# Transposing ten of sixteen token tiles with block-moving DMAs and VectorE instead of TensorE

## The chip, the cores and the metric

The kernel runs on one core of a Trainium2 chip, as one launch. The metric is the device time in microseconds (us) of one execution. Times within the kernel are counted from the start of the profiled span.

## The reference

```python
def _A_ref(x, wqkv, wo):                      # H = 32 heads of Dh = 16, W = 8, dil = 2
    q, k, v = split(x @ wqkv)
    idx = pos[:, None] - arange(W) * dil      # each token looks at itself and 7 tokens before, every second one
    logits = einsum("bhsd,bhswd->bhsw", q, k[idx]) * Dh ** -0.5
    logits = where(idx >= 0, logits, -1e9)
    o = einsum("bhsw,bhswd->bhsd", softmax(logits), v[idx])
    return o @ wo

def _B_ref(x, w1, b1, w2, b2):
    return relu(x @ w1 + b1) ** 2 @ w2 + b2

xn = _layernorm(A_x)                          # S = 2048 tokens, D = 512, F = 1792, all float32
out = A_x + _A_ref(xn, A_wqkv, A_wo) * _silu(_B_ref(xn, B_w1, B_b1, B_w2, B_b2))
```

## The kernel before

The 2048 tokens are 16 tiles of 128. Every product is made of three passes over high and low parts (`PASSES`), each operand split into a rounded high part (ScalarE, `AF.Copy`) and the remainder (a subtraction on VectorE or GpSimd). A product of one tile with one third of wqkv is 12 matmuls of 128x512.

**Stage 1** walks the tiles in pairs (a, b), a = 2, 4, ... 14; this text calls one turn of that loop a step, and (t, s) the product of tile t with third s (0 = q, 1 = k, 2 = v). A step has six products, in the order (a,0) (b,0) (a,1) (b,1) (a,2) (b,2). While it runs, the tiles of the next step are transposed, and x of the step after that is normalised:

- `mean`, `spread` and `norm` (L345, L350, L357) are the layernorm of a tile from tile 2 on: two passes of ScalarE with an accumulated sum, small operations on GpSimd, and a third pass that writes `xn`. `norm(t)` also issues the load of x of tile t + 4.
- `trans` (L376) transposes `xn` on TensorE in four blocks of 128x128 into the PSUM tile `pxT`, and ScalarE copies it to the high part of `xt`; `lowx` (L384) makes the low part on VectorE.
- `qkv` (L390) makes the product in one of four PSUM accumulators (`psA`, 4 buffers); ScalarE evacuates it to `stg`, and per pair one DMA stores it to DRAM (`sq`, `sk`, `sv`). With b stored, the pair's `xt` goes to `sx` in DRAM, for stage 2.
- `weights` loads w1 and w2 by slices f (`load_w`) through four buffers in turn (`piece`), and splits them later (`split_w`: two copies on ScalarE, two subtractions on GpSimd).

The windowed attention is a stream for VectorE (`attention`, L205), by units of 256 tokens: q, k and v of a unit are loaded back from DRAM (`load_u`), four pairs of a 128x2048 product and a reduction make the logits, softmax follows, and four more pairs make the output, stored to `so`. `pump` (L300) decides how much of this stream is put between the products: it keeps a clock for TensorE and one for VectorE, with a price for each instruction (227 ns a matmul, 150 a transpose, VectorE by elements), and issues attention until VectorE's clock is `LATE` = 3 us ahead of TensorE's. The engines' instructions then stand in the order in which they were written (`Ordered`); DMAs are placed on SP's queue by the scheduler of the language, and SP issues them strictly one after another.

**Stage 2** runs over four chunks of 512 tokens and 14 slices f: `up` (x by w1, relu, square; TensorE and ScalarE), `lowh` (the low part of h, on VectorE), `down` (h by w2), beside the rest of the attention; then the output of the attention is transposed on VectorE in 32x32 blocks (`trans_o`, L589), multiplied by wo, gated with silu and added to x. up(0,0) and up(0,1) stand already in the last step of stage 1.

Two things lie in memory where the change touches them: `zero` (L168), 14 rows that are stored ahead of k's and v's first tokens, has its own place, and so has `b2t` (L182), which is loaded in stage 1.

Of the kernel before, what the change touches and what calls it, by code (L numbers as in the profile page):

```python
# [8 lines left out]
F32 = mybir.dt.float32  # L9
FR = mybir.dt.float32r  # L10
AF = mybir.ActivationFunctionType
# [3 lines left out]
P = 128  # L15
S = 2048
D = 512
F = 1792
KT = D // P
# [4 lines left out]
HALO = (W - 1) * DIL  # L24
# [5 lines left out]
BI = 8  # L30
# [6 lines left out]

WARM = 18
WARM2 = 3

MATMUL, TRANSPOSE, DVE_FIXED, SLACK, LATE, ROOM = 227, 150, 170, 500, 3000, 1000

# [2 lines left out]
def body(ctx: ExitStack, tc: tile.TileContext, x, wqkv, wo, w1, b1, w2, b2, out):  # L45
# [3 lines left out]
    clock = {"PE": 0.0, "V": 0.0}  # L49
# [28 lines left out]
    PE, V, A, G = Ordered(nc.tensor, "PE"), Ordered(nc.vector, "V"), Ordered(nc.scalar), Ordered(nc.gpsimd)  # L78

    def not_before(t):  # L80
        clock["V"] = max(clock["V"], t)

    dma = nc.sync.dma_start

    const = ctx.enter_context(tc.tile_pool(name="const", bufs=1))
    dram = ctx.enter_context(tc.tile_pool(name="dram", bufs=1, space=bass.MemoryType.DRAM))
    att = ctx.enter_context(tc.tile_pool(name="att", bufs=1))
# [5 lines left out]
    def psA(name):  # L93
        return psum.tile([P, 512], F32, name=name, tag="acc", bufs=4)
# [4 lines left out]
    def psT(name):  # L99
        return psum.tile([P, 512], F32, name=name, tag="tp", bufs=2)  # L100
# [14 lines left out]
    ident = const.tile([P, P], F32, name="ident")  # L115
# [6 lines left out]
    px, pstg, pwq, pxT = (p1ctx.enter_context(tc.tile_pool(name=n, bufs=1)) for n in ("px", "pstg", "pwq", "pxT"))  # L122
    xins = {}
# [6 lines left out]
    def load_x(t):  # L130
        xins[t] = px.tile([P, D], F32, name=f"x{t}", tag="x", bufs=4)
        dma(xins[t], tile_rows(x, t))
# [32 lines left out]
    mhalf = const.tile([P, 1], F32, name="mhalf")  # L165
    G.memset(mhalf, -0.5)
    mask = const.tile([P, BI, W], F32, name="mask")
    zero = px.tile([HALO, 4, P], F32, name="zero")  # L168

    def constants():  # L170
        G.memset(zero, 0.0)
        for t in (sk, sv):
            dma(t[:, :HALO, :].rearrange("g h c -> h g c"), zero)
        G.memset(mask, 0.0)
        for blk in (1, 0):
            for w in range(W):
                n = max(0, min(BI, (W - 1 - w) * DIL - blk * BI))
                if n:
                    G.memset(mask[:4 * blk + 4, :n, w], -1e9)

    b1t = const.tile([P, NF], F32, name="b1t")
    b2t = const.tile([P, D], F32, name="b2t")  # L182

    sq = dram.tile([4, S, P], F32, name="sq")
    sk = dram.tile([4, HALO + S, P], F32, name="sk")
# [114 lines left out]
    def pump(margin=-SLACK):  # L300

        limit = clock["PE"] + margin
        while True:
            if coming[0] is None:
                coming[0] = next(stream, None)
            if coming[0] is None or clock["V"] + coming[0] > limit:
                break
            coming[0] = next(stream, None)
        if coming[0] is None:
            not_before(limit)  # L310
# [13 lines left out]
    def split_w(f):  # L324
        for i, r in enumerate(raws.pop(f)):
            split(w12[f][:, 0, i], w12[f][:, 1, i], r, G)


    NT = S // P
    mv, means, rs, shifts, xn, pTs, xt, xT, seen = {}, {}, {}, {}, {}, {}, {}, {}, {}  # L330

    def moments(t, st):
        mv[t] = px.tile([P, 2], F32, name=f"mv{t}", tag="mv", bufs=2)
# [5 lines left out]
    def small(name, t):  # L339
        return px.tile([P, 1], F32, name=f"{name}{t}", tag=name, bufs=3)  # L340

    def scratch(t):
        return px.tile([P, D], F32, name=f"scratch{t}", tag="scratch")

    def mean(t):  # L345
        means[t] = small("mean", t)
        A.activation(scratch(t), xins[t], AF.Copy, accum_out=means[t])
        G.tensor_scalar(means[t], means[t], -1.0 / D, None, op0=OP.mult)

    def spread(t):  # L350
        rs[t], shifts[t] = small("rs", t), small("shift", t)
        A.activation(scratch(t), xins[t], AF.Square, bias=means[t], accum_out=rs[t])
        G.tensor_scalar(rs[t], rs[t], 1.0 / D, 1e-5, op0=OP.mult, op1=OP.add)
        G.tensor_tensor(rs[t], rs[t], mhalf, op=OP.pow)
        G.tensor_mul(shifts[t], means.pop(t), rs[t])

    def norm(t):  # L357
        xn[t] = px.tile([P, D], F32, name=f"xn{t}", tag="xn", bufs=2)
        if t < 2:
            n = D // 2 if t == 0 else D  # L360
            for i in range(0, D, n):
                V.tensor_scalar(xn[t][:, i:i + n], xins[t][:, i:i + n], mv[t][:, 0:1], rs[t],
                                op0=OP.subtract, op1=OP.mult)
            del xins[t]
        else:
            A.activation(xn[t], xins.pop(t), AF.Identity, bias=shifts.pop(t), scale=rs[t])
        if t + 4 < NT:
            load_x(t + 4)

    def place(t):  # L370
        if t < TPC:
            xt[t] = xT[0][:, t]
        else:
            xt[t] = pxT.tile([P, 2, KT, P], FR, name=f"xt{t}", tag="xt", bufs=4)

    def trans(t):  # L376
        place(t)
        pTs[t] = psT(f"pxT{t}")
        for kt in range(KT):
            PE.transpose(pTs[t][:, kt * P:(kt + 1) * P], xn[t][:, kt * P:(kt + 1) * P], ident)  # L380
        seen[t] = clock["PE"] + 800
        A.activation(xt[t][:, 0], pTs[t].rearrange("p (k n) -> p k n", k=KT), AF.Copy)

    def lowx(t):  # L384
        not_before(seen.pop(t))
        V.tensor_sub(xt[t][:, 1], pTs.pop(t).rearrange("p (k n) -> p k n", k=KT), xt[t][:, 0].bitcast(F32))
# [3 lines left out]
    def qkv(t, s, between=None):  # L390
        if t % 2 == 0:
            stgs[s] = pstg.tile([P, 4, 2, P], F32, name=f"stg{t}_{s}", tag="stg", bufs=4)
        ps = psA(f"pq{t}_{s}")
        n = 0
        for kt in range(KT):
            for a, b in PASSES:
                PE.matmul(ps, xt[t][:, a, kt], wq[s][:, b, kt, :], start=n == 0, stop=n == 11)
                n += 1
            if between and kt == 1:
                between()  # L400
        A.activation(stgs[s][:, :, t % 2], ps.rearrange("p (g c) -> p g c", g=4), AF.Copy,
                     scale=0.25 if s == 0 else 1.0)
        if t % 2:
            r0 = (t - 1) * P + (0 if s == 0 else HALO)
            dst = (sq, sk, sv)[s][:, r0:r0 + UP, :].rearrange("g (p e) c -> p g (e c)", e=2)
            dma(dst, stgs[s].rearrange("p g e c -> p g (e c)"))
            done_tiles["qk" if s < 2 else "v"] = t + (s > 0)
# [24 lines left out]
    def lowh(f):  # L432
        h, ph, t = hs[f]
        not_before(t)
        V.tensor_sub(h[:, 1], ph, h[:, 0].bitcast(F32))
# [4 lines left out]
    moments(0, sts[0])  # L440
    high(*wq_parts(0, 0))
    norm(0)
    low(*wq_parts(0, 0), G)
    V.bn_stats(sts[1], xins[1])
# [4 lines left out]
    for kt in range(KT):  # L449
        PE.transpose(pT[kt // 2][:, kt * P:(kt + 1) * P], xn[0][:, kt * P:(kt + 1) * P], ident)  # L450
    for n in range(WARM2):
        PE.transpose(warm[:, :P], ident, ident)
    for kt in (0, 2):
        hi, lo = (xt[0][:, h, kt:kt + 2] for h in range(2))
        src = pT[kt // 2][:, kt * P:(kt + 2) * P].rearrange("p (k n) -> p k n", k=2)
# [52 lines left out]
    for a in range(2, NT, 2):  # L508
        b, more = a + 1, a + 2 < NT
        later = a + 4 < NT  # L510

        def weights(f):
            if 0 <= f < NKEEP:
                load_w(keep, f)
            if 0 <= f - 1 < NKEEP:
                split_w(f - 1)

        if later:
            mean(a + 4)
        qkv(a, 0)  # L520
        if more:
            trans(a + 2)
        pump(LATE)
        qkv(b, 0)
        weights(a - 5)
        if more:
            lowx(a + 2)
            trans(b + 2)
        if later:
            mean(b + 4)  # L530
        pump(LATE)
        qkv(a, 1)
        if later:
            spread(a + 4)
        if more:
            lowx(b + 2)
        pump(LATE)
        if not more:
            up(0, 0)
        qkv(b, 1)  # L540
        if later:
            spread(b + 4)
        if not more:
            pump()
            up(0, 1)
            lowh(0)
        weights(b - 5)
        pump(LATE)
        qkv(a, 2)
        if later:  # L550
            norm(a + 4)
        pump(LATE)
        qkv(b, 2)
        if later:
            norm(b + 4)
        if a == NT - 4:
            dma(b1t, b1.rearrange("(f p) -> p f", p=P))
            dma(b2t, b2[None, :].to_broadcast([P, D]))
        if a >= TPC:
            for t in (a, b):  # L560
                dma(sx[t // TPC][:, t % TPC], xt.pop(t).bitcast(F32))
        pump(LATE if more else -SLACK)
# [4 lines left out]
    p2 = ctx.enter_context(tc.tile_pool(name="p2", bufs=1))  # L567
# [60 lines left out]
        dma(tile_rows(out, t)[:, cols], z[:, cols])  # L628

    wot = p2.tile([P, 2, 4, 512], FR, name="wot")  # L630

    for c in range(NCH):
        last = c == NCH - 1
# [71 lines left out]
        else:  # L705
# [13 lines left out]
            for j in range(2, TPC):  # L719
                n = D // 2 if j == TPC - 1 else D  # L720
# [25 lines left out]
```

## Time and profile before

| | |
|---|---|
| median of 3 runs | 505.66 us (503.79 to 506.11) |
| the profiled execution | 507.61 us |
| its span | 505.8 us, 5934 instructions |
| granted TensorE clock | 0.998 |
| TensorE busy | 495.2 us (98%), 2209 matmuls |
| VectorE busy | 418.4 us (83%) |
| ScalarE busy | 214.2 us (42%) |
| GpSimd busy | 119.5 us (24%) |
| DMA | 85.64 MB, mean 169 GB/s |

In the profile PE is TensorE, PEld its weight loads, DVE VectorE, ACT ScalarE, POOL GpSimd and SP the engine that issues nearly all DMAs (SPq is its queue). A row of a timeline has its start, its length, the engine, the instruction with its tiles (written <- read), the number of merged instructions, and in brackets the idle time ahead of it with what ended it. As every instruction goes through one helper, all rows name the same line, L74; they are told apart by their tiles.

### The profile page before, as it was taken

How to read it: one execution, taken by the hardware profiler on the slowest of the kernel's cores; microseconds unless marked ns; L12 is line 12 of the kernel's file. 1: busy time of each engine (PE TensorE's matmuls, PEld its weight loads, DVE VectorE, ACT ScalarE, POOL GpSimd, SP SyncE). 2: the span in 40 equal slices, each digit the busy share in tenths (PEclk: the TensorE clock that was granted, in tenths of full speed). 3: DMA queues.
4: the chain of work that ended last, by engine and by line, in shares of the span. 5: the costliest groups of instructions: out<-in, count | busy, mean ns of one | idle time of the engine just before them, and what ended most of it. 6: DMA issues, size and time to landing. Idle time of an engine off the chain costs nothing.

```text
span 505.8 us, 5934 instructions
## 1 busy us (share of the span) xinstructions
PE 495.2 (98%) x2209; PEld 406.4 (80%) x2209; DVE 418.4 (83%) x327; ACT 214.2 (42%) x393; POOL 119.5 (24%) x127
## 2 busy tenths in 40 slices
PE   7999989999999999999999999999999999999996
PEld 5788878878787888888888888888888878888885
DVE  5208999999999999997799999589998859995244
ACT  4955275573333556431722442263224136223321
POOL 3622076484000399700203000020200002120000
PEclk9999999999999999999999999999999999999999
DMA  8888787689947774643323515344241612112022
GB/s 293 248 260 296 250 322 230 237 312 338 323 141 238 210 227 141 193 165 158 114 65 144 198 41 183 140 123 158 75 173 33 238 44 84 62 64 83 0 84 84
DMA packets 45064, 85.64 MB, mean 169 GB/s; under 512 B 4988, under 2 KB 28908, under 8 KB 42220
## 3 DMA queue, kind: packets, MB, share of 16 engines
q1 hardware_dynamic: 44172, 78.98, 47.2%
q10 hardware_dynamic: 864, 6.29, 3.4%
q8 instruction: 17, 0.28, 0.2%
q14 instruction: 11, 0.09, 0.1%
HBM read 57.94 MB, written 27.32 MB: 169 GB/s over the span
## 4 chain that ended last, share of the span: by engine, by line
PE 70%; DVE 17%; issue 4%; ACT 3%; DMA 3%; POOL 3%; POOLq 0%; ACTq 0%; DVEq 0%
PE pb L74 30%; PE ph L74 29%; PE pw L74 9%; DVE L L74 5%; DVE pr L74 5%; DMA x<-in_A_x 3%; PE pq L74 3%; DVE v L74 2%; DVE pv L74 2%; ACT scratch L74 1%; POOL rs L74 1%; POOL wq L74 1%; DVE xt L74 1%; ACT stg L74 1%; DVE xn L74 1%
## 5 line engine op out<-in xcount | busy, mean ns | idle before, releaser
L74 PE MATMUL pb<-w,h 128*128 128x512 f32 x672 | 160.6, 389 | 0.0
L74 PEld LDWEIGHTS pb<-w,h 128*128 128x128 f32 x672 | 126.1, 188 | 26.2
L74 PE MATMUL ph<-xU,w 128*128 128x512 f32 x504 | 120.7, 390 | 0.0
L74 ACT ACTIVATE ph<-ph,b1t 128x512 f32<-128x512 f32 x56 | 37.0, 661 | 193.0 <-PE ph L74 187.3
L74 PEld LDWEIGHTS ph<-xU,w 128*128 128x128 f32 x504 | 94.3, 188 | 20.6 <-DVE h L74 0.9
L74 PE MATMUL pq<-wq,xt 128*128 128x512 f32 x432 | 101.6, 392 | 0.9 <-ACT stg L74 0.9
L74 PEld LDWEIGHTS pq<-wq,xt 128*128 128x128 f32 x432 | 80.3, 188 | 17.8 <-ACT stg L74 1.4
L74 DVE TENSOR_TENSOR pr<-k,q 128x2048 f32<-128x2048 f32 x32 | 77.0, 2407 | 14.0 <-DMA x<-in_A_x 13.6
L74 DVE TENSOR_TENSOR pv<-v,L 128x2048 f32<-128x2048 f32 x32 | 75.6, 2362 | 0.5
L74 DVE TENSOR_TENSOR h<-ph,h 128x512 fp32r<-128x512 f32 x56 | 38.4, 685 | 42.8 <-ACT ph L74 42.8
L74 DVE TENSOR_REDUCE L<-pr 128x128 f32<-128x2048 f32 x32 | 73.0, 2282 | 0.7
L74 DVE TENSOR_REDUCE v<-pv 128x256 f32<-128x2048 f32 x32 | 72.9, 2280 | 0.6
L74 POOL TENSOR_TENSOR z<-z,xr 128x512 f32<-128x512 f32 x12 | 21.2, 1778 | 219.3 <-DVE z L74 212.5
L74 PE MATMUL pw<-wot,oT 128*128 128x512 f32 (+1 forms) x204 | 45.5, 376 | 0.0
L74 ACT ACTIVATE stg<-pq 128x512 f32<-128x512 f32 x48 | 28.3, 595 | 35.6 <-PE pq L74 35.6
L74 PEld LDWEIGHTS pw<-wot,oT 128*128 128x128 f32 x204 | 36.8, 188 | 7.1
L74 PE MATMUL ph<-xT,w 128*128 128x512 f32 x168 | 40.6, 391 | 0.1
L74 PEld LDWEIGHTS ph<-xT,w 128*128 128x128 f32 x168 | 31.5, 188 | 7.1 <-DVE h L74 0.5
L74 PE MATMUL pq<-wq,xT 128*128 128x512 f32 x144 | 36.2, 402 | 0.6 <-DVE wq L74 0.4
L74 POOL TENSOR_TENSOR w<-w1r,w 128x512 fp32r<-128x512 f32 x14 | 22.1, 1580 | 60.9 <-DMA rwo<-in_A_wo 49.6
L74 POOL TENSOR_TENSOR w<-w2r,w 128x512 fp32r<-128x512 f32 x14 | 34.5, 2466 | 0.0
L74 ACT ACTIVATE h<-ph 128x512 fp32r<-128x512 f32 x56 | 33.7, 601 | 1.8
(54 smaller groups left out, 325.7 us busy)
## 6 DMA issues: line engine op xcount, KB each, us to landing
k<-sk SPq DMA_DIRECT2D x8, 1408.0 KB, 8.2
v<-sv SPq DMA_DIRECT2D x8, 1408.0 KB, 7.9
sx<-xt SPq DMA_DIRECT2D x12, 512.0 KB, 4.8
xU<-sx ACTq DMA_DIRECT2D x6, 1024.0 KB, 5.7
x<-in_A_x SPq DMA_DIRECT2D x16, 256.0 KB, 6.0
sq<-stg SPq DMA_DIRECT2D x8, 512.0 KB, 5.2
q<-sq SPq DMA_DIRECT2D x8, 512.0 KB, 4.2
sk<-stg SPq DMA_DIRECT2D x8, 512.0 KB, 4.9
```

The source lines that it names most:

```text
L74: return tc.keep_in_program_order(f(*a, **k))
```

## The change

Tiles 0 to 5 are transposed as before. For tiles 6 to 15 (`TURN = 6`), `norm` writes a pair of tiles into one tile of SBUF with the columns in another order, `shuffle` moves its blocks of 32 partitions to other partitions with 16 DMAs of 32 partitions x 1 KB, and `trans` then transposes 32x32 blocks on VectorE straight into `pxT`. What follows (ScalarE's copy, `lowx`) is as before, but stands two products later for these tiles. `spread` and `norm` of a step stand two products earlier. `zero` takes the buffer of the first q, and `b2t` is loaded at the start of stage 2 into memory that stage 1 had.

```diff
+TURN = 6
...
-    zero = px.tile([HALO, 4, P], F32, name="zero")
     def constants():
+        zero = att.tile([P, BI, P], F32, name="zero", tag="q")[:HALO, :4]
         G.memset(zero, 0.0)
...
-    b2t = const.tile([P, D], F32, name="b2t")
...
     def norm(t):
-        xn[t] = px.tile([P, D], F32, name=f"xn{t}", tag="xn", bufs=2)
+        if t < TURN:
+            xn[t] = px.tile([P, 2, D], F32, name=f"xn{t}", tag="xn", bufs=2)[:, 0]
+        elif t % 2 == 0:
+            xn[t] = px.tile([P, 4, 2, P], F32, name=f"xn{t}", tag="xn", bufs=2)
...
+        elif t < TURN:
+            A.activation(xn[t], xins.pop(t), AF.Identity, bias=shifts.pop(t), scale=rs[t])
         else:
-            A.activation(xn[t], xins.pop(t), AF.Identity, bias=shifts.pop(t), scale=rs[t])
+            A.activation(xn[t // 2 * 2][:, :, t % 2].rearrange("p a (k c) -> p k a c", k=KT),
+                         xins.pop(t).rearrange("p (k a c) -> p k a c", a=4, k=KT),
+                         AF.Identity, bias=shifts.pop(t), scale=rs[t])
...
+    def shuffle(t):
+        src = xn.pop(t)
+        xb[t] = px.tile([P, 4, 2, P], F32, name=f"xb{t}", tag="xn", bufs=2)
+        for b in range(4):
+            for a in range(4):
+                dma(xb[t][32 * a:32 * a + 32, b], src[32 * b:32 * b + 32, a])
+
     def trans(t):
         place(t)
         pTs[t] = psT(f"pxT{t}")
-        for kt in range(KT):
-            PE.transpose(pTs[t][:, kt * P:(kt + 1) * P], xn[t][:, kt * P:(kt + 1) * P], ident)
-        seen[t] = clock["PE"] + 800
+        if t < TURN:
+            for kt in range(KT):
+                PE.transpose(pTs[t][:, kt * P:(kt + 1) * P], xn[t][:, kt * P:(kt + 1) * P], ident)
+            seen[t] = clock["PE"] + 800
+        else:
+            V.transpose(out=pTs[t].rearrange("p (k b n) -> p b k n", k=KT, n=32),
+                        in_=xb[t // 2 * 2][:, :, t % 2].rearrange("p b (k c) -> p b k c", k=KT))
+            seen[t] = clock["V"] + 800
         A.activation(xt[t][:, 0], pTs[t].rearrange("p (k n) -> p k n", k=KT), AF.Copy)
...
         qkv(a, 0)
-        if more:
+        if a + 2 < TURN:
             trans(a + 2)
+        if later:
+            spread(a + 4)
+            mean(b + 4)
         pump(LATE)
         qkv(b, 0)
         weights(a - 5)
-        if more:
+        if a + 2 < TURN:
+            lowx(a + 2)
+            trans(b + 2)
+        elif more:
+            trans(a + 2)
+        if later:
+            norm(a + 4)
+            spread(b + 4)
+        pump(LATE)
+        qkv(a, 1)
+        if a + 2 < TURN:
+            lowx(b + 2)
+        elif more:
             lowx(a + 2)
             trans(b + 2)
         if later:
-            mean(b + 4)
-        pump(LATE)
-        qkv(a, 1)
-        if later:
-            spread(a + 4)
-        if more:
-            lowx(b + 2)
+            norm(b + 4)
+            shuffle(a + 4)
         pump(LATE)
...
         qkv(b, 1)
-        if later:
-            spread(b + 4)
+        if TURN <= a + 2 < NT:
+            lowx(b + 2)
...
         qkv(a, 2)
-        if later:
-            norm(a + 4)
         pump(LATE)
         qkv(b, 2)
-        if later:
-            norm(b + 4)
         if a == NT - 4:
             dma(b1t, b1.rearrange("(f p) -> p f", p=P))
-            dma(b2t, b2[None, :].to_broadcast([P, D]))
...
+    b2t = p2.tile([P, D], F32, name="b2t")
+    dma(b2t, b2[None, :].to_broadcast([P, D]))
```

More of the change, by code (lines that the diff above doesn't have):

```diff
@@ L329, in body @@
     NT = S // P
-    mv, means, rs, shifts, xn, pTs, xt, xT, seen = {}, {}, {}, {}, {}, {}, {}, {}, {}
+    mv, means, rs, shifts, xn, xb, pTs, xt, xT, seen = ({} for _ in range(10))
     def moments(t, st):
```

## The prediction

> **What bounds the kernel now.** I read the page first, then TensorE's timeline, then the waits, and last the engines by stage.
>
> ```profile
> PE 495.2 (98%) x2209; PEld 406.4 (80%) x2209; DVE 418.4 (83%) x327; ACT 214.2 (42%) x393; POOL 119.5 (24%) x127
> PE 70%; DVE 17%; issue 4%; ACT 3%; DMA 3%; POOL 3%; POOLq 0%; ACTq 0%; DVEq 0%
> ```
>
> TensorE is busy for 98% of the span, and the chain that ended last lies on it for 70%. The timeline of TensorE says where it is not at its peak (start, length, what, and in brackets the wait ahead):
>
> ```profile
> 46.20 2.91 PE L74 MATMUL pq<-wq,xt 128*128 128x512 f32 x12
> 48.95 0.60 PE L74 MATMUL pxT<-ident,xn 128*128 128x128 f32 x4
> 49.31 3.02 PE L74 MATMUL pq<-wq,xt 128*128 128x512 f32 x12
> 52.16 0.60 PE L74 MATMUL pxT<-ident,xn 128*128 128x128 f32 x4
> ...
> 67.84 0.66 PE L74 MATMUL pxT<-ident,xn 128*128 128x128 f32 x4 [1.45 <-ACT xn L74]
> ...
> 102.75 0.66 PE L74 MATMUL pxT<-ident,xn 128*128 128x128 f32 x4 [0.18 <-ACT xn L74]
> ...
> 132.98 11.18 PE L74 MATMUL pq<-wq,xt 128*128 128x512 f32 x48 [0.95 <-ACT stg L74]
> 144.00 2.94 PE L74 MATMUL ph<-xT,w 128*128 128x512 f32 x12
> ...
> 163.53 3.01 PE L74 MATMUL ph<-xT,w 128*128 128x512 f32 x12
> ```
>
> 48 matmuls run from 132.98 to 144.00, so a product of 12 takes 2.75. From 46.20, where step 4 begins, to 163.53, where up(0,3) begins, lie 117.3 us with 40 products (36 of q/k/v, three of up, one of down): 110.0. The other 7.3 are ten groups of transposes, each 0.36 (48.95 to 49.31) plus the 0.10 by which the next product is longer (49.31 to 52.16 is 2.85), 4.6 together, and the waits in brackets, 2.6. Behind 163.53 the chain has no other engine until the last tiles; what TensorE gains or loses before it reaches the end whole. 7.3 is the most that the change can give.
>
> VectorE and the DMA engines in the same stretch (busy time of PE, PEld, DVE, ACT, POOL, then clock, DMA share, GB/s):
>
> ```profile
> 63.40:82.35 18.95, 17.50 (x82) 14.24 (x81) 18.74 (x11) 13.26 (x29) 15.20 (x18) 1.00 0.78 278
> 99.60:117.20 17.60, 17.42 (x82) 14.17 (x81) 17.43 (x12) 13.53 (x29) 15.70 (x20) 1.00 0.94 326
> 117.20:134.50 17.30, 16.35 (x77) 13.21 (x76) 17.09 (x12) 5.07 (x10) 2.20 (x1) 1.00 0.91 318
> ```
>
> VectorE has no gap here, and the DMA engines are 91 to 94% busy from 99.6 to 134.5; 326 at 0.94 makes 347 GB/s when full. So three resources are near their limit at once, and the change takes from one and gives to the other two.
>
> **The change, part by part.** Off TensorE: 4.6, and the waits of 2.6 if nothing new takes their place.
>
> On VectorE: ten transposes.
>
> ```profile
> 485.12 1.31 DVE L74 STREAM_TRANSPOSE pT<-oq 128x512 f32<-128x512 f32 x2
> 39.71 2.29 DVE L74 TENSOR_TENSOR pr<-k,q 128x2048 f32<-128x2048 f32 x1 [13.62 <-DMA x<-in_A_x]
> 59.13 0.68 DVE L74 TENSOR_TENSOR xt<-pxT,xt 128x512 fp32r<-128x512 f32 x1
> 162.79 0.68 DVE L74 TENSOR_TENSOR h<-ph,h 128x512 fp32r<-128x512 f32 x1
> L74 DVE TENSOR_REDUCE v<-pv 128x256 f32<-128x2048 f32 x32 | 72.9, 2280 | 0.6
> 496.10 5.75 PE L74 MATMUL pw<-wot,oT 128*128 128x512 f32 x36
> ```
>
> One is 0.65 (the same form, SBUF to PSUM): 6.5 in all. VectorE runs from 39.71 to the end of lowh(1), 163.4, without a gap: 123.7. In the changed order as built, lowh(1) has ahead of it one value reduction (2.3, the row of reductions), one softmax normalisation (1.9, three small operations like xt's 0.68) and two products with their reductions (4 x 2.3) fewer, as the planner's clock for TensorE shrinks by 40 x 150 ns and VectorE's grows. 123.7 - 13.4 + 6.5 = 116.8, so lowh(1) ends at 156.5 at the earliest; up(0,3) needs it, and TensorE without waits is there at 46.2 + 110.0 = 156.2. The two engines are level, and each wait of VectorE now counts. At the end the attention's last reduction stands three f steps (3 x 5.4) later. Now the last oq loads, issued by 466.4 (below), land near 470 and are read at 485.1; later by 16 they land near 486, and TensorE wants these tiles at 496.1. I cost it at nothing; without that cover each us of lateness would count.
>
> The zeros in q's buffer: the first q load must wait for the zeros' stores and stands behind the first k load.
>
> ```profile
> 30.86 0.54 SPq L202 DMA_DIRECT2D k<-sk  x1
> 31.49 0.55 SPq L406 DMA_DIRECT2D sv<-stg  x1
> 41.01 0.53 SPq L202 DMA_DIRECT2D v<-sv  x1
> SPq L202 <- DMA sv<-stg: 5.2, 1, 5.2
> ```
>
> The sv store, issued right behind k, had landed only at 41.0 (v waits for it). q takes that place: VectorE starts at 41.0, 1.3 late (0 if transfers overtake; 2.5 if both share the rate).
>
> The block moves: 16 DMAs of 32 KB per pair, five pairs, on SP's queue.
>
> ```profile
> 166.43 3.77 SPq L649 DMA_DIRECT2D rwo<-in_A_wo  x8
> 464.70 1.73 SPq L587 DMA_DIRECT2D oq<-so  x4
> DMA to landing us min/median/max: 2.4/3.4/5.4
> SPq L132 <- DMA wqraw<-in_A_wqkv: 1.5, 3, 0.9
> ```
>
> SP needs 1.73/4 = 0.43 (oq) to 3.77/8 = 0.47 (rwo) for one, so 6.9 for a pair; oq's 128 KB land in 2.4 at best (third row). The last row: x loads wait three times for weight loads with whose data they have nothing to do. In the program each DMA carries one of eight completion semaphores in turn, so a DMA isn't issued before the eighth ahead of it has landed. Sixteen small ones are two such rounds: the first waits for the eight large transfers ahead, and behind them the DMA engines carry only 0.5 MB in some 6 us.
>
> Each pair's round trip: transpose 0.65, one VectorE operation and lowx 2.9, second transpose 0.65, ScalarE's copy 0.6 and norm 0.8, issues 6.9, landing 2.4: 14.9, against six products, 16.5. It fits by 1.6 with nothing ahead in the queue, and that is what decides.
>
> The Trainium skill's page "DMA: Bandwidth & Descriptors", Rules for kernel authors, speaks against the change: small transfers should be coalesced, since under 64 KB one pays mostly overhead. The rows agree on the shape: oq's 128 KB take 3.4, k's 1408 KB 8.2. By the page's fit (Anatomy of one DMA) 32 KB would land in about 2.1, an estimate from it; a round trip would be 14.6 and the sum the same, since w2r decides it. No run shows a 32 KB move between partitions yet.
>
> ```profile
> k<-sk SPq DMA_DIRECT2D x8, 1408.0 KB, 8.2
> sk<-stg SPq DMA_DIRECT2D x8, 512.0 KB, 4.9
> oq<-so SPq DMA_DIRECT2D x32, 128.0 KB, 3.4
> L74 ACT ACTIVATE xn<-x,shift,rs 128x512 f32<-128x512 f32 x14 | 11.3, 808 | 3.3 <-POOL shift L74 3.3
> L74 ACT ACTIVATE xt<-pxT 128x512 fp32r<-128x512 f32 x12 | 7.1, 592 | 0.0
> 113.30 0.62 ACT L74 ACTIVATE w<-w1r 128x512 fp32r<-128x512 f32 x1
> ```
>
> Now the steps in time, in the changed orders of ScalarE, VectorE and SP. ScalarE takes in order: the copy of xt waits for VectorE's transpose, and behind it stand norm, the softmax's exp, the splits of w and the evacuations that free TensorE's four accumulators.
> Step 6 (46.2 + 6 x 2.75 = 62.7): transpose(6) stands where lowx(6) stood, 59.1 + 1.3 = 60.4. Behind its copy ScalarE does norm(8), spread(9), exp and the evacuation of (4,1), done at 64.3; TensorE wants that buffer at 62.7. Wait 1.7.
> Tile 8: the k load of unit 1 stands behind the x load that norm(8) frees (62.4), and lands at 70 to 71. The seventh block move waits for it by the rule of eight; with ten more at 0.43 and 2.4 to land, transpose(8) can start at 77.5, where VectorE is ready at 74.4. VectorE loses 3.1, lowx(9) and lowx(11) come 0.5 and 0.7 late for TensorE, and the split of w3, loaded behind the moves, holds an evacuation 1.4. Together 2.6; the buffer of (10,1) comes 0.4 late. Step 12 begins at 46.2 + 24 x 2.75 + 4.7 = 116.9.
> Last pair: SP is through with tile 12's moves at about 109. Ahead of tile 14's then stand k (1408 KB), six transfers of 512 KB like sk's (sk, q, sv, two sx, sq) and three weight slices of half that: 5.4 MB, at 347 GB/s until 124.7; w2r lands at about 126.5. ScalarE comes to that split behind the copy of tile 13 and norm(15), at about 118.5 (at 113.3 before, with its data there), and blocks; behind it is the evacuation that (12,1) needs, wanted at 116.9 + 5.5 = 122.4 and done at 128.7. Wait 6.3 (0 if the data is there by 118; 10 at the 278 GB/s of the first row of stages). Tile 14's moves land at about 134; VectorE, ready at 127.7, waits 6.3 beside it, not on top: (14,0) begins at 128.7 + 4 x 2.75 = 139.7 either way.
>
> The statistics' new places cost nothing by themselves: ScalarE is idle for 58% of the span. b2t isn't read before the first gate, a whole pass over f later. ScalarE's two more table loads fall where it waits for ph.
>
> Sum on TensorE: -4.6 - 2.6 + 1.7 + 2.6 + 0.4 + 6.3 = **+3.8**. The profiled execution took 507.61 (span 505.8), 1.95 over the median of the runs shown, 505.66: a like execution 511.4, the median 509.5.
>
> **The rivals.** *The moves are hidden* (faster): transfers overtake one another, or the queue drains sooner, and w2r and the blocks are there when asked for. Against it are 91 to 94% of DMA share; for it, that ScalarE's split at 113.30 has no wait in its row. Then VectorE's chain decides, 39.7 + 116.8 + 1.3 + about 1 = 158.8 against 163.5: -4.7, **501.0**; with q on time as well -6, never under -7.3 (498.4). It decides from the point where w2r lands before 118.5 and tile 14's blocks before 128.
>
> *SP slows in the deep queue* (slower still). Where the backlog was deepest, SP needed far more for one issue:
>
> ```profile
> 108.98 1.33 SPq L561 DMA_DIRECT2D sx<-xt  x1
> 120.04 1.02 SPq L320 DMA_DIRECT2D w1r<-in_B_w  x1
> ```
>
> At 1.1 instead of 0.43 the last 16 moves take 10.7 longer: tile 14 comes at 145, tile 15's low half 7.3 of VectorE's work later, and step 14 begins at about 149 instead of 139.7: 9.5 more, **519**. It decides once 16 issues take over 11.
>
> That the change does not do what it says is excluded by the built order: 40 matmuls gone, ten transposes and 80 DMAs there.
>
> **How the numbers follow.** About 0.5% (2.5 us) is what a measurement of this kernel can tell from no change. Forecast 0.55, its own range 505 to 513 (the last wait between 2 and 10): slower 0.38, same 0.15, faster 0.02. Hidden moves 0.30: faster 0.26, same 0.04. Slow issue 0.15: slower. Faster 0.28, same 0.19, slower 0.53. The range takes in most of the hidden case and the upper bound of the last wait: 499.5 to 514.
>
> **What would show it.** Right: pxT gone from TensorE behind 46 us; ten transposes of pxT at 0.65; a wait of TensorE on stg near 122, with ScalarE waiting for w2r; VectorE waiting for xb ahead of tiles 8 and 14; the first pr at about 41. Wrong: no ScalarE wait on w, TensorE's up(0,3) before 161, or block moves landing within 9 us of norm throughout. If TensorE waits behind 170, for h or at the end, I missed where the attention went.

## The result and the profile after

| | time, median | ratio to before, 95% interval |
|---|---|---|
| before | 505.88 us (503.79 to 506.17) | |
| after | 532.83 us (531.80 to 533.12) | 1.0552 [1.0526, 1.0578] |

The change makes the kernel 5.5% slower. The forecast was 509.5, in a range from 499.5 to 514: the direction held, the size did not. The profiled execution took 532.79, its span is 531.0, and the granted clock fell from 0.998 to 0.971.

The page after, TensorE's busy share and the chain that ended last:

```profile
PE 499.9 (94%) x2169; PEld 410.2 (77%) x2169; DVE 422.5 (80%) x337; ACT 217.2 (41%) x395; POOL 108.5 (20%) x127
...
PE 68%; DMA 10%; DVE 9%; SPq 4%; issue 3%; POOL 3%; ACT 3%; ACTq 0%; DVEq 0%; POOLq 0%
PE ph L76 29%; PE pb L76 27%; PE pw L76 6%; PE pq L76 6%; DMA sx<-xt 5%; DVE pr L76 3%; SPq L392 3%; DVE L L76 2%; DMA x<-in_A_x 2%; POOL rs L76 1%; DVE z L76 1%; DMA w2r<-in_B_w 1%; DMA oq<-so 1%; POOL w L76 1%; ACT xn L76 1%
```

Forty matmuls are gone, and TensorE is still busy for longer. On the chain, DMA has grown from 3% to 10%, SP's queue is new with 4%, and two names stand there that were not there before: the stores to sx (5%) and the block moves (SPq L392, 3%). TensorE's timeline, with the waits in brackets:

```profile
46.42 32.83 PE L76 MATMUL pq<-wq,xt 128*128 128x512 f32 x144
83.08 19.17 PE L76 MATMUL pq<-wq,xt 128*128 128x512 f32 x72 [3.83 <-ACT stg L76]
105.62 18.21 PE L76 MATMUL pq<-wq,xt 128*128 128x512 f32 x72 [3.37 <-ACT stg L76]
135.93 21.13 PE L76 MATMUL pq<-wq,xt 128*128 128x512 f32 x84 [12.10 <-ACT stg L76]
161.85 8.19 PE L76 MATMUL pq<-wq,xt 128*128 128x512 f32 x24 [4.79 <-ACT stg L76]
...
189.17 2.88 PE L76 MATMUL ph<-xT,w 128*128 128x512 f32 x12
```

up(0,3) begins at 189.17 instead of 163.53, 25.6 later, and the span ended 25.2 later: all of the loss arises in stage 1. From 46.42 to 189.17 lie 142.75 us with the same 40 products, 110.0 at 2.75 each. Of the other 32.75, the four waits for `stg` are 24.1; the remaining 8.6 are matmuls that ran slower. In each of the steps 8, 10, 12 and 14 one evacuation came late from ScalarE. What ScalarE had been waiting for (engine and tile that waited, what ended it, us in total, times, longest):

```profile
ACT xt L76 <- DMA sx<-xt: 33.7, 4, 10.5
...
PE pq L76 <- ACT stg L76: 24.1, 4, 12.1
...
DVE xt L76 <- ACT xt L76: 21.5, 5, 9.9
...
DVE pxT L76 <- DMA xb<-xn: 12.8, 4, 4.3
...
ACT w L76 <- DMA w2r<-in_B_w: 6.6, 1, 6.6
```

The first row is the one to read: ScalarE's copy into `xt`, which the change left as it was but for its place, waits for stores to sx. `xt` has four buffers; that of tile t is free for tile t + 4 only when its store to sx has landed. SP's queue shows where that store now stands:

```profile
62.91 11.51 SPq L392 DMA_DIRECT2D xb<-xn  x16
74.52 0.53 SPq L430 DMA_DIRECT2D sk<-stg  x1
75.15 0.45 SPq L430 DMA_DIRECT2D sv<-stg  x1
75.65 2.28 SPq L590 DMA_DIRECT2D sx<-xt  x2
```

The sixteen moves hold the queue for 11.5 us, and the stores of tiles 4 and 5 go out behind them at 75.65. In the kernel before they went out as soon as their tiles were done:

```profile
42.63 0.33 SPq L561 DMA_DIRECT2D sx<-xt  x1
...
45.42 0.62 SPq L561 DMA_DIRECT2D sx<-xt  x1
```

Their place in the queue has changed as well as the length of the holds. In the run stats_only below, the same program with no moves, the scheduler lets them go at 42.48 and 47.67. Here the two tiles were complete at 40.6 and 43.4, but two sets of moves (42.01 to 53.62 and 62.91 to 74.42) and nine other DMAs stand ahead of their stores.

The copies of tiles 8 and 12 then wait on ScalarE (its timeline, with a split that waits for w2r between them):

```profile
80.55 0.60 ACT L76 ACTIVATE xt<-pxT 128x512 fp32r<-128x512 f32 x1 [10.50 <-DMA sx<-xt]
...
124.60 0.63 ACT L76 ACTIVATE w<-w2r 128x512 fp32r<-128x512 f32 x1 [6.64 <-DMA w2r<-in_B_w]
...
133.39 0.60 ACT L76 ACTIVATE xt<-pxT 128x512 fp32r<-128x512 f32 x1 [8.16 <-DMA sx<-xt]
```

ScalarE works in order, so the evacuations behind such a copy wait with it: TensorE starts at 83.08 behind the first and at 135.93 behind the last. The stages are the three that were shown of the kernel before (busy time of PE, PEld, DVE, ACT, POOL, then clock, DMA share, GB/s):

```profile
63.40:82.35 18.95, 15.85 (x70) 12.78 (x69) 11.87 (x9) 6.70 (x15) 7.45 (x7) 0.98 0.64 222
...
99.60:117.20 17.60, 14.23 (x56) 11.35 (x55) 14.93 (x10) 9.80 (x21) 8.31 (x9) 0.90 0.60 186
117.20:134.50 17.30, 6.63 (x30) 5.16 (x28) 3.77 (x4) 2.50 (x5) 2.91 (x4) 0.76 0.81 278
```

The DMA engines carry less than before in each (0.94 fell to 0.60 in the second). What is held up is the queue in which SP issues, not the engines behind it.

### The profile page after: what moved, and what is told of

Its sections match the earlier page's. It is cut to its first block, busy times and chain, and to the rows that moved or that the text cites. A ratio compares the mean times of both kernels' runs of the same rounds, so it can differ in the third digit from the quotient of the medians.

```text
span 531.0 us, 5965 instructions
## 1 busy us (share of the span) xinstructions
PE 499.9 (94%) x2169; PEld 410.2 (77%) x2169; DVE 422.5 (80%) x337; ACT 217.2 (41%) x395; POOL 108.5 (20%) x127
## 2 busy tenths in 40 slices
DMA packets 48906, 88.29 MB, mean 166 GB/s; under 512 B 6268, under 2 KB 32748, under 8 KB 46060
## 4 chain that ended last, share of the span: by engine, by line
PE 68%; DMA 10%; DVE 9%; SPq 4%; issue 3%; POOL 3%; ACT 3%; ACTq 0%; DVEq 0%; POOLq 0%
PE ph L76 29%; PE pb L76 27%; PE pw L76 6%; PE pq L76 6%; DMA sx<-xt 5%; DVE pr L76 3%; SPq L392 3%; DVE L L76 2%; DMA x<-in_A_x 2%; POOL rs L76 1%; DVE z L76 1%; DMA w2r<-in_B_w 1%; DMA oq<-so 1%; POOL w L76 1%; ACT xn L76 1%
## 5 line engine op out<-in xcount | busy, mean ns | idle before, releaser
L76 PE MATMUL pq<-wq,xt 128*128 128x512 f32 x432 | 108.1, 413 | 24.1 <-ACT stg L76 24.1
L76 PEld LDWEIGHTS pq<-wq,xt 128*128 128x128 f32 x432 | 87.0, 202 | 44.7 <-ACT stg L76 25.8
L76 DVE TENSOR_TENSOR pr<-k,q 128x2048 f32<-128x2048 f32 x32 | 74.5, 2327 | 11.9 <-POOL rs L76 11.4
L76 POOL TENSOR_TENSOR w<-w1r,w 128x512 fp32r<-128x512 f32 x14 | 25.3, 1808 | 72.1 <-DMA rwo<-in_A_wo 53.4
L76 ACT ACTIVATE ph<-ph 128x512 f32<-128x512 f32 x56 | 33.3, 595 | 0.0
```

The lines of the kernel that those rows point to most:

```text
L76: return tc.keep_in_program_order(f(*a, **k))
```

## The experiments

The expectations below name these explanations:

- A: the moves hold SP's queue, and what stands behind them comes late, sx first.
- B: the moved blocks themselves land late for VectorE.
- C: the ten transposes cost VectorE too much.
- D: the statistics, which stand two products earlier, cost the time.
- E: the traffic of the moves costs it, whoever issues them.
- W: as A, but it is the weight loads behind the moves that come late.

The times, each beside runs of the kernel before on the same chip (504.7 to 506.2):

| run | time | ratio, 95% interval |
|---|---|---|
| no_moves | 499.43 | 0.9886 [0.9849, 0.9922] |
| stats_only | 504.24 | 0.9975 [0.9957, 0.9994] |
| moves_unused | 532.64 | 1.0543 [1.0511, 1.0576] |
| unused_half | 513.28 | 1.0152 [1.0123, 1.0181] |
| sx_early | 523.05 | 1.0361 [1.0320, 1.0402] |
| unused_sx_early | 522.01 | 1.0335 [1.0305, 1.0366] |
| sx_early_w_pool | 515.01 | 1.0187 [1.0158, 1.0216] |
| pool_queue | 523.13 | 1.0357 [1.0324, 1.0391] |
| split_sx_early | 508.90 | 1.0068 [1.0046, 1.0090] |
| dram_hop | 504.21 | 0.9976 [0.9958, 0.9994] |
| dram_hop_sx_early | 499.59 | 0.9890 [0.9863, 0.9918] |

### Which part of the change costs

**no_moves**

```diff
-                        in_=xb[t // 2 * 2][:, :, t % 2]...
+                        in_=xn[t // 2 * 2][:, :, t % 2]...
...
-            shuffle(a + 4)
```

> The changed kernel without its 80 moves: VectorE transposes the 32x32 blocks of xn where they lie, so that the blocks stand in the wrong places of the transposed tile (this part of the computation is left out); every other instruction stays. Theories A and B: SP's queue is free, nothing waits for moved blocks, and what is left is ten transpose groups less on TensorE: 499-505 us. Theory C (the ten transposes on VectorE are themselves too dear, or push the attention's instructions back): over 510 us. Theory D (the moved statistics): over 515 us.

499.43: the transposes on VectorE, with TensorE freed of its own, are worth having by themselves. C falls. (This run leaves out the moving of the blocks, so it is a bound and no kernel to use.)

**stats_only**

```diff
-TURN = 6
+TURN = 16
...
-            shuffle(a + 4)
```

> The changed kernel with all tiles transposed on TensorE and no moves: of the change only the statistics and normalisations two products earlier stay (and the places of two constants). Theories A, B and C: within 1% of the kernel before, 502-509 us. Theory D (the moved statistics delay ScalarE's evacuations): over 515 us.

504.24: D falls. From here to no_moves are 4.8 us, ten groups of transposes; the forecast had 4.6 for them.

**moves_unused**

```diff
-TURN = 6
+TURN = 16
...
-                dma(xb[t][32 * a:32 * a + 32, b], src[32 * b:32 * b + 32, a])
+                u = both[t + a // 2]
+                n = slice(256 * (a % 2), 256 * (a % 2) + 256)
+                dma(u[32 * (3 - b):32 * (3 - b) + 32, 1, n], u[32 * b:32 * b + 32, 0, n])
```

> As the kernel with the moved statistics alone (all tiles transposed on TensorE), but with the 80 moves of 32 partitions x 1 KB put back at their places on SP's queue; they go into halves of the xn buffers that nothing reads, so no instruction uses the moved data. Theory A: SP's queue is held as in the changed kernel, sx and the weights go out as late, ScalarE waits over 15 us for sx, 518-535 us. Theory B: no engine waits for the moved blocks, so 502-509 us.

532.64, as slow as the change itself. Moves that no instruction uses cost 28.4 us over stats_only. The waits of this run:

```profile
ACT xt L76 <- DMA sx<-xt: 46.0, 5, 18.0
...
PE pq L76 <- ACT stg L76: 20.0, 5, 9.7
```

B is not needed for a loss of this size; the moves make it alone, by the queue that they hold (A, W) or by their traffic (E). Like for like the moves cost 28.4 here and 33.4 in the changed kernel (532.83 against no_moves). No run divides the other 5.0 between late blocks and whatever else differs there.

**unused_half**

```diff
-            for a in range(4):
+            for a in range(b % 2, 4, 2):
```

> The kernel of the unused moves with eight moves per pair of tiles in place of sixteen; sx at its old place. Theory A: the queue is held for 5 to 6 us per pair; sx lands some 5 us earlier, and ScalarE had that much to spare in part, so less than half of the loss of 28 us over the kernel with the moved statistics alone remains: 505-514 us. If each issue costs by itself and nothing hides it: half the loss, 516-520 us.

513.28: half of the moves cost 9.0 over stats_only, a third of the full 28.4. Part of the hold is hidden, as A has it, though ScalarE still waits 26.4 us for sx:

```profile
ACT xt L76 <- DMA sx<-xt: 26.4, 5, 11.5
...
PE pq L76 <- ACT stg L76: 6.1, 2, 4.3
```

### What is held up behind the moves

**sx_early**

```diff
     def lowx(t):
...
+        if t >= TPC:
+            dma(sx[t // TPC][:, t % TPC], xt[t].bitcast(F32))
...
-        if a >= TPC:
-            for t in (a, b):
-                dma(sx[t // TPC][:, t % TPC], xt.pop(t).bitcast(F32))
```

> The changed kernel, but each store of a finished transposed tile to sx is put right behind the subtraction that completes the tile, so that on SP's queue the stores of tiles 4 and 5 stand ahead of the first sixteen moves and the later ones at least one set of moves earlier than now. The moves, their queue and VectorE's transposes stay. Theory A (the moves hold SP's queue, the sx stores behind them give xt's four buffers back late, ScalarE stands at its copy into xt for 33.7 us, and TensorE waits for its evacuations): ScalarE's waits on sx fall under 8 us, TensorE's waits for stg fall from 24.1 us to under 9, the time falls from 532.8 to 506-516. Theory B (the moved blocks themselves reach VectorE late): VectorE's waits on xb stay near 12.8 us and the time at 527-534. Theory D (the moved statistics): no change.

523.05: ScalarE's waits on sx are gone, and 9.8 us with them. A's numbers were wrong all the same (506 to 516, with TensorE's waits for stg under 9, where 15.7 were left): two other waits came up in their place, which the sx wait had covered.

```profile
ACT xt L76 <- DVE pxT L76: 25.7, 5, 9.4
ACT w L76 <- DMA w1r<-in_B_w: 24.8, 3, 12.5
...
PE pq L76 <- ACT stg L76: 15.7, 3, 7.2
DVE pxT L76 <- DMA xb<-xn: 14.4, 4, 7.2
```

The copy of xt now waits for VectorE's transpose, which waits for the blocks (B), and the splits wait for weights (W). Two runs take one of them away each.

**unused_sx_early**: moves_unused with sx early as above.

> The kernel of the unused moves (all tiles transposed on TensorE, 80 moves on SP's queue that nothing reads) with the sx stores right behind the subtractions. No engine can wait for moved blocks here, and sx is out of the way, so what is left of the loss is what the held queue does to the other loads and stores, the weights above all. If sx and the late blocks are the whole loss (theory A with B for the rest): 505-510 us, ScalarE's waits on w under 5 us. Theory W (the weight loads behind the moves are the larger rest, as forecast for w2r): 513-523 us, ScalarE's waits on w over 12 us.

522.01, W's side, with no blocks to wait for:

```profile
ACT w L76 <- DMA w1r<-in_B_w: 25.0, 3, 10.3
...
ACT xn L76 <- DMA xn<-xn: 11.8, 2, 8.5
PE pq L76 <- ACT stg L76: 11.7, 3, 7.0
```

The second row blurs it: norm wants a buffer that the unused moves still read, which theory W did not have in it and which this construction brought in. So the run shows that the weights are late enough to hold ScalarE for 25 us, not that they make the 17.8 us over stats_only alone.

**sx_early_w_pool**

```diff
-        dma(r1.rearrange(...
-        dma(r2, w2[f * P:(f + 1) * P, :])
+        q = nc.gpsimd.dma_start if f < NKEEP else dma
+        q(r1.rearrange(...
+        q(r2, w2[f * P:(f + 1) * P, :])
```

> The run with sx early, and the loads of w1r and w2r for f = 0 to 5 issued from GpSimd's queue in place of SP's; the moves stay on SP's. Theory W (the rest of the loss in sx_early, 523.0 us, is the weights behind the moves): ScalarE's waits on w (24.8 us there) fall under 6 us and the time to 505-512 us. Theory B (the rest is the blocks themselves that land late, 14.4 us of VectorE's waits there): waits on xb stay over 10 us and the time at 516-524 us.

515.01, between the two theories' numbers: ScalarE's waits for weights are gone, and 8.0 us of sx_early's time with them (W); the waits for blocks remain (B). The waits:

```profile
ACT xt L76 <- DVE pxT L76: 39.7, 9, 10.1
...
DVE pxT L76 <- DMA xb<-xn: 19.5, 5, 7.9
...
PE pq L76 <- ACT stg L76: 8.9, 4, 4.5
```

So one cause, the held queue, reaches ScalarE by three ways: the buffer of xt by sx, the splits by the weights, the copy of xt by the blocks. They lie beside each other, and each removal uncovers the next.

### Other ways to move the blocks

**pool_queue**

```diff
-                dma(xb[t][32 * a:32 * a + 32, b], src[32 * b:32 * b + 32, a])
+                nc.gpsimd.dma_start(xb[t][32 * a:32 * a + 32, b], src[32 * b:32 * b + 32, a])
```

> The changed kernel with its 80 moves issued from GpSimd's queue; everything else stays. Theory A (what costs is that SP's queue is held for 10 to 12 us per pair of tiles): SP's queue runs as without the moves (499.4 us), ScalarE's waits on sx and on the weights are gone, and with the blocks landing in time the result is 499-506 us. If GpSimd takes more than 0.9 us for one issue, sixteen take over 14 us, the blocks reach VectorE late and its waits on xb rise over 13 us: 506-518 us. Theory E (the moves cost by their traffic or by crossing other transfers, whoever issues them): 520-533 us.

523.13, far from A's 499 to 506 and within E's 520 to 533. SP is free, and sx and most weights are on time, but the moves of one pair take GpSimd (its timeline) as long as they took SP:

```profile
62.60 4.08 POOL L392 DMA_DIRECT2D xb<-xn  x8 [1.65 <-DVE xt L76]
69.53 3.91 POOL L392 DMA_DIRECT2D xb<-xn  x8 [2.84 <-DMA xb<-xn]
```

Eight issues of 0.50, a wait until earlier moves have landed, eight more: 62.60 to 73.44. Each move lands later than from SP's queue (median 4.8 against 1.9), as the view of the moved tile says, and VectorE waits 20.7 us for blocks:

```profile
DMA to landing us min/median/max: 1.6/4.8/9.5
```

By TensorE's waits the late blocks are not the larger part. GpSimd works in order too, and its own small operations stand behind the moves, `mean` among them, which ScalarE's second pass over x needs:

```profile
ACT scratch L76 <- POOL mean L76: 35.1, 6, 12.6
```

In the changed kernel that wait is 7.1. ScalarE gets on at 95.56 and 121.99 after 9.27 and 12.57 us of it, and TensorE's two longest waits for `stg` in this run, 3.24 and 7.64 of 14.5, end right behind, at 97.67 and 124.09. So the number is E's, but the trace shows a held engine again, GpSimd in place of SP. The condition in the expectation was on the issue time, which was short.

**split_sx_early**: `(dma if b % 2 else nc.gpsimd.dma_start)(...)`, and sx early.

> The changed kernel with half of its moves on SP's queue and half on GpSimd's (eight each per pair of tiles), and the sx stores right behind the subtractions as in the run with sx early. Theory A: SP is held for 5 to 6 us per pair, the blocks are complete some 5 us earlier than now, and VectorE's waits on xb fall under 5 us: 499-508 us. Theory E (traffic): over 515 us.

508.90, 0.9 above A's range, with VectorE's waits for blocks as A has them, at 2.7 us; ScalarE waits 6.7 for w1r. The same eighty moves that cost 523.05 from SP alone (sx_early) cost 14.2 less from two queues, which speaks against E. The executions spread more than others (505.06 to 510.43, ten), and the profiled one was the fastest of them, so its trace doesn't explain the median.

**dram_hop**

```diff
-        for b in range(4):
-            for a in range(4):
-                dma(xb[t][32 * a:32 * a + 32, b], src[32 * b:32 * b + 32, a])
+        hop = dram.tile([P, 4, 2 * P], F32, name=f"hop{t}")
+        dma(hop.rearrange("p a x -> p (a x)"), src.rearrange("p a e c -> p (a e c)"))
+        for a in range(4):
+            dma(xb[t][32 * a:32 * a + 32].rearrange("p b e c -> p b (e c)"),
+                hop[:, a].rearrange("(b p) x -> p b x", p=32))
```

> The changed kernel with the sixteen moves of 32 KB in place of one store of the pair's 512 KB to DRAM and four loads of 128 KB back, on SP's queue; sx stays at its old place. Theory A: five issues take SP some 3 us instead of 10 to 12, but the four loads stand at SP's head until the store has landed, 4 to 6 us; sx is still late by part of that: 505-520 us. Theory E (traffic; this moves twice the bytes): over 530 us.

504.21, a little under A's range. ScalarE still waits 20.5 us for sx, as the stores keep their late place in the queue: the first two go out at 69.52, behind the second pair's blocks.

**dram_hop_sx_early**: the same with sx early.

> The hop through DRAM (one store and four loads on SP's queue in place of sixteen moves) with the sx stores right behind the subtractions. Theory A: ScalarE's waits on sx gone, VectorE's waits on xb under 8 us: 500-512 us, and at least 5 us below the run with sx early alone (523.0). Theory E (traffic): over 525 us.

499.59: 1.1% faster than the kernel before, and level with no_moves, where no block is moved at all. The late place of the sx stores, with short holds ahead of them, had cost 4.6 us (504.21 to 499.59). SP's queue and the stages of this run:

```profile
80.31 1.13 SPq L391 DMA_DIRECT2D hop<-xn  x1
81.53 0.39 SPq L434 DMA_DIRECT2D sk<-stg  x1
82.01 0.73 SPq L414 DMA_DIRECT2D sx<-xt  x1
85.15 1.90 SPq L393 DMA_DIRECT2D xb<-hop  x4
```

```profile
82.35:99.60 17.25, 17.25 (x78) 14.29 (x77) 17.11 (x12) 10.03 (x22) 11.72 (x13) 1.00 1.02 325
99.60:117.20 17.60, 17.60 (x79) 14.32 (x77) 17.46 (x14) 11.20 (x23) 8.09 (x11) 1.00 1.01 343
```

Five issues take SP 3.0 us of a pair (1.13 and 1.90) instead of 11.5, and sk and sx go out while the store to DRAM lands. The DMA engines are full here (shares of 1.0, 90.90 MB in all against 88.29 after), and TensorE has no gap at a clock of 1.00. E falls as the cause of the loss: a full set of DMA engines cost nothing, and a held queue with engines at 0.60 cost 27 us. What the eighty small moves cost by themselves when nothing stands behind them, no run shows; split_sx_early is 9.5 us above no_moves.

## Why the prediction was wrong in size

**The step that failed** is the pair's round trip, and what I let hang on SP's queue. I followed the blocks and the weight loads through SP's queue, and counted the sx stores only as bytes ahead of w2r. That a store also gives a buffer back, and that ScalarE's next copy stands behind it, is in none of my steps; it held ScalarE for 33.7 us in four waits. I asked of the queue only which loads stand in it, not which stores.

**The term that was mis-sized** is the issue: 0.43 to 0.47 from the oq and rwo rows, 6.9 for a pair. Measured on the changed kernel:

```profile
L392 SPq DMA_DIRECT2D xb<-xn x80: 507/589/1578, 42.0 to 147.0; - x80
L76 DVE STREAM_TRANSPOSE pxT<-xb x10: 712/717/727, 57.1 to 152.7; 128x512 f32<-128x512 f32 x10
DMA to landing us min/median/max: 1.8/1.9/6.1
```

A median of 0.589, and 11.51 for the sixteen quoted above, 0.72 each with the gaps; 1.2 of the 11.51 are a wait for the k load, as the prediction's rule of eight has it. With 11.5 for 6.9 my own round trip is 19.5 against six products of 16.5; with the 10.0 of the shortest set it is 18.0. It did not fit in any pair. unused_half shows what that is worth: a hold about half as long cost 9.0 instead of 28.4.

**The rival "SP slows"** was the nearest, at 519 with 0.15. It put 1.1 us on an issue and was to decide from 11 us for sixteen on; measured were 10.0 to 11.6. But I gave it only to the last pair, whose sixteen took 10.14, and let it act by the blocks alone, for 9.5 us. In the runs the hold came with every pair, and sx and the weights were late by it too.

**Point by point.** Right: the transposes went from TensorE for 4.6 (4.8 between stats_only and no_moves); the hidden case, 501.0 and with q on time 499.7, is what no_moves and dram_hop_sx_early give (499.4, 499.6); VectorE waits for the blocks of tiles 8 and 14 (4.34 and 0.97, where 3.1 and 6.3 were forecast, but also 3.84 and 3.62 for tiles 10 and 12); the statistics' places cost nothing; behind 186 TensorE waits for nothing, so the late attention is hidden. Right by luck: ScalarE's wait for w2r, which took 6.64 us and ended at 124.60, where the forecast has it from 118.5 to 126.5. The forecast had SP through with tile 12's moves at 109 and the load behind 5.4 MB of transfers. SP began those moves only then, and issued the load behind them (L322):

```profile
109.06 10.02 SPq L392 DMA_DIRECT2D xb<-xn  x16
119.18 1.13 SPq L430 DMA_DIRECT2D sk<-stg  x1
120.40 0.46 SPq L322 DMA_DIRECT2D w2r<-in_B_w  x1
```

It landed 4.2 us later. So the time is nearly right, and the mechanism is the held queue again. Wrong: the DMA engines' share as the limit (0.60 to 0.81 where I had 0.91 to 0.94); the transpose on VectorE (0.717 where I had 0.65); and VectorE's start, which came earlier, not 1.3 later:

```profile
37.72 2.29 DVE L76 TENSOR_TENSOR pr<-k,q 128x2048 f32<-128x2048 f32 x1 [11.43 <-POOL rs L76]
```

2.0 before the old 39.71, and without worth, as VectorE was soon waiting for ScalarE (21.5 us in all).

**The cost of a wait beyond its length**, the 8.6 us, was in no step either. In moves_unused, where transposes on TensorE keep the products apart, the rows show it:

```profile
134.12 5.10 PE L76 MATMUL pq<-wq,xt 128*128 128x512 f32 x12 [9.68 <-ACT stg L76]
141.29 4.61 PE L76 MATMUL pq<-wq,xt 128*128 128x512 f32 x12 [2.06 <-ACT stg L76]
...
146.09 3.02 PE L76 MATMUL pq<-wq,xt 128*128 128x512 f32 x12
```

The first product behind a wait of 9.68 takes 5.10 instead of some 2.9. In the changed kernel the granted clock is 0.50 from 83.08, where the first wait ends, to 88.00, and 1.00 again from 90.00; over the stages with such waits it is 0.76 to 0.90. The Trainium skill's page "TensorE: Matmul & The Clock Gate", Part 1, says that TensorE falls to half rate after an idle window of about 3.4 us and needs as long under load to come back; the trace agrees on the half rate, behind waits of 3.4 to 12.1 in the changed kernel. On the length of the window the runs agree only in part: behind a wait of 2.71 in moves_unused a product took 4.50, and behind one of 3.24 in pool_queue 3.04.

The Trainium skill's page "DMA: Bandwidth & Descriptors", section "Issuing engines are not separate DMA queues", says that issuing from several engines only saves sequencer time, "which is usually small relative to the DMA itself". Here the traces differ on the size: one issue took 0.72 us with the gaps where a move lands in 1.9, and sixteen held SP for 10.0 to 11.6 us. With half of the moves on a second queue the kernel took 14.2 us less (split_sx_early against sx_early). The fit in the section "Anatomy of one DMA", from which the prediction has its 2.1 us, is given by the Trainium skill for DMAs issued from GpSimd, and the changed kernel issues its moves from SP; they landed in 1.9 from SP's queue, and in 4.8 from GpSimd's in pool_queue (medians).

## What to carry to other kernels

Price a DMA that is added to an in-order queue by what stands behind it: loads, stores that give a buffer back to an engine that nobody thinks of as waiting for DMA, and, where a computing engine issues it, that engine's own work. Look also at where the scheduler puts the old DMAs now. Count issues times their measured length against the queue's free time per step; when that overflows, several waits lie beside one another, and taking away the longest shows only the next. Here, five large DMAs per pair through DRAM, with more bytes on full DMA engines, cost nothing where sixteen small ones cost 5.5%.

## What the runs showed of the hardware that was not expected

- A move of 32 partitions x 1 KB between SBUF partitions takes SP 0.589 us to issue (median of 80), longer than a load of 128 KB from DRAM in dram_hop (0.430, median of 20). No run shows why.
- From GpSimd's queue (pool_queue) the same move is issued in 0.50 us, but lands in 4.8 (median) instead of 1.9.
- In moves_unused the product behind a wait of TensorE of 9.68 us took 5.10 us, and the next, behind a further wait of 2.06, took 4.61, where others take some 2.9.
